# Order of the token-mixing work inside the value projection: PV products one by one, two transposes moved ahead, the short tile fourth of five

## The chip, the core and the metric

The kernel runs on one NeuronCore of one Trainium2 chip. The core has five engines that run side by side and wait for each other by semaphores: TensorE (PE, matrix products, results into PSUM), VectorE (DVE), ScalarE (ACT), GpSimd (POOL) and SyncE (SP, which issues most DMAs). The metric is device time in microseconds (us) of one execution; lower is better.

## The reference

Eight images (b = 0 to 7) of 576 tokens and 512 channels go through three blocks, all in float32:

```python
q_s = exp(q - max(q, -1)); q_s /= sum(q_s, -1) + 1e-9          # per head, over 64 channels
k_s = exp(k - max(k, 2));  k_s /= sum(k_s, 2) + 1e-9           # over the 576 tokens
x   = q_s @ (k_s^T @ v)                                        # (576, 512) per image
h   = gelu_tanh(x @ w_in)                                      # 512 -> 1024
u, v = h[:, :512], h[:, 512:]
v_n = (v - mean) / sqrt(var + 1e-6) * g_ln                     # over the 512 channels
y   = x + (u * (w_sg @ v_n + b_sg)) @ w_out                    # w_sg mixes tokens
t   = y + (y^T @ U @ V)^T                                      # rank 32, over tokens
out = t + relu(t @ w_ch1) @ w_ch2                              # 512 -> 2048 -> 512
```

## The kernel before

Every float32 operand of a product is split into a high part `h` (float32r) and a low rest `l`, and a product is made of three: h·h, h·l, l·h. ACT makes the high part by a copy, DVE or POOL the low part by a subtraction (`low`).

The first three blocks run image by image in one loop over `b`; the last block (`ch1`, `ch2`) runs over 512 columns of all tokens after it. An image's pass has these stages on PE: `emit_xT` (px, four of them: x transposed), `emit_Vh` (pv: the v half of x @ w_in, one tile of 128 tokens each for t = 0 to 3 and a short tile of 64 tokens, t = NT = 4), `emit_Uh` (pu, four: the u half), `emit_S` (pS: token mixing by w_sg), then `emit_kv` and `emit_qT` of the next image and `emit_y` (py). The rank-32 product of an image is not finished in its own pass. Its transposes `emit_yT` (pt, from tile yt) for t = 0 and 1 stand between the px of the next image, and the transposes for t = 2, 3, 4, the product with U (`emit_U`, pp, nine products) and the four products with V (`emit_PV`, pw, two products each) stand inside the pv stage of the next image. So the pv stage of images 1 to 7 holds pieces of the image before.

What follows a pv tile: ACT takes gelu of it (ge), DVE takes mean and variance (`stats`: bn_stats, bn_aggr, add), POOL the power -0.5 (mv), DVE the shift (sh), ACT normalises in place and copies the high part (vh), POOL subtracts the low part (vl). The short tile is computed with high and low rows side by side, so its pv is first copied by ACT, then added by DVE (tile ge, 64 partitions), then put through gelu, and its low part is made by DVE into the other half of vh4. After a pw, DVE adds it to yt, and SP sends yt to DRAM (u2d).

Beside this the key maximum of the next image is found: DVE folds the key tiles (`k_fold`, km, in two halves of two operations), PE transposes km (`k_max`, pm), DVE reduces it (mx, mh, ml), POOL makes two diagonal matrices of it (diag), and PE spreads it over all partitions (`k_spread`, pb, between the second and the third pu); ACT copies that to kmx, DVE subtracts it from the keys, ACT takes exp.

What sets the order: PE's order is the order of the code everywhere. For images 1 to 6 DVE's order is that of the code too; ACT, POOL and SP are ordered ahead of time by a scheduler with a time model of its own. For image 0 DVE, ACT, POOL and SP, and for image 7 ACT, follow the code. On the chip each engine runs its list strictly in that order.

PSUM has eight banks: `ps2` holds three tiles of two banks (tag "big"), handed out in turn to px, pv, pw, pu, pS, py, and to the transposes t = 2 and 3; `ps1` holds two tiles of one bank for the transposes t = 0, 1, 4, for pp, pm, pb and pk. A new tile waits until the one three (or two) places before it in the same pool has been read by its last reader.

Of the kernel before, what the change touches and what calls it, by code (L numbers as in the profile page):

```python
# [22 lines left out]
def fused_kernel(tc, q, k, v, w_in, g_ln, w_sgT, b_sg, w_out, U, V, w_ch1, w_ch2, outT):  # L23
# [4 lines left out]
    NT = S // P  # L28
# [18 lines left out]
    def mm(out, lhsT, rhs, first, last):  # L47
        pe.matmul(out, lhsT, rhs, start=first, stop=last)  # L48
# [456 lines left out]
    vh = {}  # L505
    ln = {}

    def emit_Vh(b, t):
        xh, xl, xr, _ = x_t[b]
        pv = ps2.tile([P, 1024], F32, tag="big", name="pv")[:, 0:F]  # L510
        cols = slice(F, 2 * F)
        for kc in range(NC):
            if t < NT:
                a, l = xh[:, kc, t * P : (t + 1) * P], xl[:, kc, t * P : (t + 1) * P]
                mm(pv, a, wi_h[:, kc, cols], kc == 0, False)
                mm(pv, a, wi_l[:, kc, cols], False, False)
                mm(pv, l, wi_h[:, kc, cols], False, kc == NC - 1)
            else:
                a = xr[:, kc].rearrange("p j r -> p (j r)")
                mm(pv, a, wi_h[:, kc, cols], kc == 0, False)  # L520
                mm(pv, a, wi_l[:, kc, cols], False, kc == NC - 1)
        ge = tmpp.tile([P, F], F32, tag="ge", name="ge", bufs=3)
        ln[b, t] = ge
        if t < NT:
            act.activation(ge, pv, AF.Gelu_apprx_tanh)
        else:
            copy(ge[0:R], pv[64 : 64 + R])
            tt(dve, ge[0:R], pv[0:R], ge[0:R], ALU.add)
            act.activation(ge[0:R], ge[0:R], AF.Gelu_apprx_tanh)
# [11 lines left out]
    def emit_ln(b, t):  # L541
        ge, mv = ln.pop((b, t))
        n = TR[t]
        shift = tmpp.tile([P, 1], F32, tag="sh", name="sh", bufs=4)
        dve.scalar_tensor_tensor(
            out=shift[0:n], in0=mv[0:n, 0:1], scalar=-1.0, in1=mv[0:n, 1:2], op0=ALU.mult, op1=ALU.mult
        )
        act.activation(ge[0:n], ge[0:n], AF.Identity, bias=shift[0:n], scale=mv[0:n, 1:2])
        h = wrk.tile([P, F], F32R, tag=f"vh{t}", name=f"vh{t}")
        if t < NT:  # L550
            l = wrk.tile([P, F], F32R, tag=f"vl{t}", name=f"vl{t}")
            copy(h, ge)
            low(pool, l, ge, h)
            vh[b, t] = (h, l)
        else:
            copy(h[0:R], ge[0:R])
            low(dve, h[64 : 64 + R], ge[0:R], h[0:R])
            vh[b, t] = h
# [58 lines left out]
    def emit_yT(b, t):  # L617
        n = TR[t]
        if t not in (2, 3):
            pt = ps1.tile([P, C], F32, tag="ps1", name="pt1")  # L620
        else:
            pt = ps2.tile([P, 1024], F32, tag="big", name="pt1")[:, 0:C]
        for c in range(NC):
            pe.transpose(pt[0:n, c * P : (c + 1) * P], y_t[b][:, c, t * P : t * P + n], ident)
        h = wrk.tile([P, C], F32R, tag=f"vh{t}", name=f"yh{t}")
        if t < NT:
            l = wrk.tile([P, C], F32R, tag=f"vl{t}", name=f"yl{t}")
            copy(h, pt)
            low(dve, l, pt, h)
            yn[b, t] = (h, l)  # L630
        else:
            copy(h[0:R], pt[0:R])
            low(dve, h[64 : 64 + R], pt[0:R], h[0:R])
            yn[b, t] = (h,)
# [98 lines left out]
    def more(n):  # L733

        for _ in range(n):
            while pieces and len(loaded) < 3:
                loaded.append(pieces.popleft())
                if not loaded[-1].loaded:
                    loaded[-1].load()
            while stores:  # L740
                stores.popleft()()
            if loaded:
                begun.append(loaded.popleft())
                begun[-1].start()
            if len(begun) > 1 or (begun and not loaded and not pieces):
                merged.append(begun.popleft())
                merged[-1].merge()
            if len(merged) > 1 or (merged and not begun):
                merged.popleft().split()
# [13 lines left out]
    spread = [mid] * B  # L763
# [69 lines left out]
    for b in range(B):  # L833
        nxt = b + 1 if b + 1 < B else None
        part = in_order(*order.get(b, (dve,)))
        part.__enter__()

        if not nxt:
            close_att()
            p2a, close_p2a = opened("p2a", side="right")  # L840
            load_u(p2a, 0)
        if nxt:
            load_k(nxt)
            fold = k_fold(nxt)
        for t in range(NT + 1):
            emit_Vh(b, t)
            if nxt:
                with behind(dve):
                    for t2 in ((0, 1), (2, 3), (4,), (), ())[t]:
                        q_max(nxt, t2)  # L850
                    if t in (2, 3):
                        next(fold)
                        next(fold)
            if t < NT:
                stats(b, t)
            more(spread[b][0][t])
            if t > 0:
                emit_ln(b, t - 1)
            if t == NT:
                stats(b, t)  # L860
            if b == 0 and t > 0:
                sum_x(b, t - 1)
            if b > 0:
                for t2 in {0: (2,), 1: (3, 4)}.get(t, ()):
                    emit_yT(b - 1, t2)
            if t == 2 and b > 0:
                for t2 in range(NT + 1):
                    emit_U(b - 1, t2)
            if t in (3, 4) and b > 0:
                for c in range(2 * t - 6, 2 * t - 4):  # L870
                    emit_PV(b - 1, c)

        if nxt:
            k_max(nxt)
        for f in range(NF):
            if nxt and f == 2:
                k_spread(nxt)
            if b == 0:
                more(spread[b][1][f])
            emit_Uh(b, f)  # L880
            if f == 0:
                emit_ln(b, NT)
                if nxt:
                    load_v(nxt)
            if nxt:
                for t in ((0, 1), (2, 3, 4), (), ())[f]:
                    q_sub(nxt, t, pool if b == 0 and t > 1 else dve)
                for t in ((), (), (0, 1), (2, 3, 4))[f]:
                    k_sub(nxt, t)
            if b > 0:  # L890
                more(spread[b][1][f])
            if not nxt and f == 1:
                load_w(p2a, 0)
                split_u(p2a, 0)
        if nxt:
            for t in range(NT + 1):
                q_exp(nxt, t)
            k_exp(nxt)
            for t in range(NT + 1):
                q_sum(nxt, t)  # L900
            q_total(nxt)
            for t in range(NT + 1):
                q_norm(nxt, t, dve if t < 2 else pool)

        for f in range(NF):
            emit_S(b, f)
            if f > 0:
                split_G(b, f - 1)
            if f == NF - 1:
                split_G(b, f)  # L910
            if not nxt and f == NF - 1:
                close_wi()
                p2b, close_p2b = opened("p2b", 3, side="right")
                for fc in (1, 2):
                    load_w(p2b, fc)

                def early(fc):
                    ch1(0, fc, ps2.tile([P, 1024], F32, tag="big", name="ph")[:, 0:BLK], p2b)

                early(0)  # L920
            more(spread[b][2][f])
        if nxt:
            emit_kv(nxt)
            emit_qT(nxt, 0)
            emit_qT(nxt, 1)
            norm_kv(nxt)
        for c in range(NC):
            more(spread[b][3][c])
            emit_y(b, c)
            if nxt and 0 < c < 3:  # L930
                emit_qT(nxt, 1 + c)
                if c == 2 and b + 2 < B:
                    load_q(b + 2)
        if nxt:
            emit_xT(nxt, 0)
            emit_xT(nxt, 1)
            emit_yT(b, 0)
            emit_xT(nxt, 2)
            emit_yT(b, 1)
            emit_xT(nxt, 3)  # L940
        else:
            early(1)
            more(99)
            for t in range(NT + 1):
                emit_yT(b, t)
            for t in range(NT + 1):
                emit_U(b, t)
            early(2)
            for c in range(NC):
                emit_PV(b, c)  # L950
        if b < B - 1:
            part.__exit__(None, None, None)
# [75 lines left out]
```

## Time and profile before

| | |
|---|---|
| median of 3 runs | 1430.74 us (1428.48 to 1434.74) |
| the profiled execution | 1432.9 us |
| its span, first to last instruction | 1431.1 us |
| PE busy | 1370.5 us, 96% of the span |
| DVE, ACT, POOL busy | 631.9, 485.2, 348.9 us |
| mean granted TensorE clock | 0.981 of full speed |

The profiled execution is 1.8 us longer than its span and 2.2 us above the median. Images 0 to 7 take the first 645 us or so of the span, the last block the rest. A busy PE counts overlapping products, so PE's losses are read from the starts of its instructions: back to back, products of 512 columns start 0.23 us apart.

### The profile page before, as it was taken

To read this page: it belongs to the slowest core of one execution; us is meant where nothing else is said; L and a number is where in the kernel's file an instruction comes from. 1 tells how busy PE (TensorE), PEld (TensorE's weight loads), DVE (VectorE), ACT (ScalarE), POOL (GpSimd) and SP (SyncE) were. 2 spreads that over 40 slices of the span, in tenths; PEclk is the share of its full clock that TensorE was granted. 3 is DMA by queue.
4 is the path that set the end of the run, shared out by engine and by line. 5 is a ranking of instruction groups with operands and counts; after the bars stand their busy time and mean duration, and the time that the engine had idled before them with its cause. 6 is when DMAs were issued, how large, how long until landed. Compare 5 with 4: busy or idle time off the path is not lost.

```text
span 1431.1 us, 19023 instructions
## 1 busy us (share of the span) xinstructions
PE 1370.5 (96%) x7672; PEld 1180.5 (82%) x7672; DVE 631.9 (44%) x1140; ACT 485.2 (34%) x838; POOL 348.9 (24%) x384
## 2 busy tenths in 40 slices
PE   3688999999999999998999999999999999999998
PEld 2488898989898988897888888888888888888887
DVE  6787868686868687654521111112111111111111
ACT  3455757575757565522411111111111111111110
POOL 5864343434343334423400001010010100101000
PEclk8789999999999999999999999999999999999999
DMA  7324333323232422448210010101001010010000
GB/s 244 104 83 125 92 118 90 125 82 124 84 125 83 125 82 90 143 148 297 75 59 0 0 60 0 59 1 40 20 0 59 0 60 0 1 59 1 30 0 30
DMA packets 72056, 104.42 MB, mean 73 GB/s; under 512 B 5920, under 2 KB 34592, under 8 KB 71968
## 3 DMA queue, kind: packets, MB, share of 16 engines
q1 hardware_dynamic: 69088, 92.72, 20.4%
q0 software_dynamic: 2880, 10.49, 2.2%
q8 instruction: 60, 0.98, 0.3%
q14 instruction: 28, 0.23, 0.0%
HBM read 73.83 MB, written 29.36 MB: 72 GB/s over the span
## 4 chain that ended last, share of the span: by engine, by line
PE 82%; DVE 6%; ACT 4%; DMA 3%; POOL 2%; issue 2%; SPq 0%; ACTq 0%; DVEq 0%; POOLq 0%
PE acc L48 27%; PE ph L48 27%; PE pS L48 7%; PE py L48 7%; PE pv L48 5%; PE pu L48 5%; DMA stg<-in_w_ch_dram 1%; PE pt L453 1%; PE pk L48 1%; PE pp L48 1%; ACT xh L57 1%; ACT x L57 1%; DMA u2d<-yt 1%; DVE stg L173 1%; POOL qt L51 1%
## 5 line engine op out<-in xcount | busy, mean ns | idle before, releaser
L48 PE MATMUL acc<-hh,w 128*128 128x512 f32 x1152 | 379.3, 390 | 0.0
L48 PE MATMUL ph<-uh,w 128*128 128x512 f32 x1152 | 378.1, 389 | 0.0
L706 DVE SCALAR_TENSOR_TENSOR hl<-ph,hh 128x512 fp32r<-128x512 f32 x144 | 99.4, 691 | 569.5 <-ACT hh L705 569.5
L705 ACT ACTIVATE hh<-ph 128x512 fp32r<-128x512 f32 x144 | 86.0, 597 | 639.7 <-PE ph L48 639.7
L48 PEld LDWEIGHTS acc<-hh,w 128*128 128x128 f32 x1152 | 217.1, 188 | 45.2
L48 PEld LDWEIGHTS ph<-uh,w 128*128 128x128 f32 x1152 | 216.5, 188 | 45.0
L48 PE MATMUL acc<-hl,w 128*128 128x512 f32 x576 | 225.2, 391 | 4.0 <-DVE hl L706 4.0
L48 PE MATMUL ph<-ul,w 128*128 128x512 f32 x576 | 224.1, 389 | 0.0
L51 POOL TENSOR_TENSOR ul<-u,uh 128x512 fp32r<-128x512 f32 x32 | 40.6, 1300 | 566.4 <-ACT uh L57 566.4
L48 PEld LDWEIGHTS acc<-hl,w 128*128 128x128 f32 x576 | 108.7, 189 | 26.9 <-DVE hl L706 4.4
L48 PEld LDWEIGHTS ph<-ul,w 128*128 128x128 f32 x576 | 108.0, 188 | 22.4
L174 ACT ACTIVATE f<-stg 128x256 f32<-128x256 f32 (+2 forms) x91 | 39.2, 434 | 68.9 <-DVE stg L173 30.7
L48 PE MATMUL py<-gh,wo_h 128*128 128x288 f32 x256 | 57.9, 308 | 2.9 <-DVE gt L590 2.9
L48 PE MATMUL pu<-xh,wi_h 128*128 128x288 f32 x256 | 57.5, 307 | 2.1 <-DVE yt L51 2.1
L48 PE MATMUL pv<-wi_h,xh 128*128 128x512 f32 x128 | 53.0, 414 | 3.6 <-ACT xh L57 3.6
L48 PE MATMUL pu<-xh,wi_l 128*128 128x288 f32 x256 | 55.9, 300 | 0.6 <-POOL wi_l L51 0.6
L48 PE MATMUL pv<-wi_h,xl 128*128 128x512 f32 x128 | 52.6, 411 | 3.7 <-DVE xl L51 3.7
L48 PE MATMUL pu<-xl,wi_h 128*128 128x288 f32 x256 | 55.9, 300 | 0.0
L48 PE MATMUL py<-gh,wo_l 128*128 128x288 f32 x256 | 55.8, 300 | 0.0
L48 PE MATMUL py<-gl,wo_h 128*128 128x288 f32 x256 | 55.7, 300 | 0.0
L48 PE MATMUL pS<-sg_h,vh 128*128 128x288 f32 x256 | 54.8, 296 | 0.3 <-ACT ut L570 0.3
L48 PE MATMUL pS<-sg_h,vl 128*128 128x288 f32 x256 | 54.7, 295 | 0.0
(148 smaller groups left out, 2206.9 us busy)
## 6 DMA issues: line engine op xcount, KB each, us to landing
stg<-in_w_ch_dram SPq DMA_DIRECT2D x64, 256.0 KB, 2.6
wd<-chw SPq DMA_DIRECT2D x40, 256.0 KB, 2.9
w<-wd POOLq DMA_DIRECT2D x20, 512.0 KB, 7.2
u2d<-yt SPq DMA_DIRECT2D x32, 288.0 KB, 2.1
u<-u2d SPq DMA_DIRECT2D x9, 1024.0 KB, 5.3
out_dram<-res SPq DMA_DIRECT2D x36, 256.0 KB, 2.1
vt<-in_v_dram SPq DMA_DIRECT2D x32, 256.0 KB, 6.7
qt<-in_q_dram SPq DMA_DIRECT2D x7, 1024.0 KB, 6.2
```

Of the source, the lines that this page charges most:

```text
L48: pe.matmul(out, lhsT, rhs, start=first, stop=last)
L51: return eng.tensor_tensor(out=out, in0=a, in1=b, op=op)
L57: act.activation(out, src, AF.Copy)
L173: eng.tensor_scalar(out=hi, in0=hi, scalar1=F64_MOST, scalar2=-F64_MOST, op0=ALU.min, op1=ALU.max)
L174: act.activation(t, hi, AF.Prelu, scale=F64_SCALE, alpha=F64_SIGN)
L453: pe.transpose(pt[:, t * P : t * P + n], qt[0:n, t, c * P : (c + 1) * P], ident[0:n, 0:n])
L705: act.activation(a, ph, AF.Relu)
L706: dve.scalar_tensor_tensor(out=l, in0=ph, scalar=0.0, in1=as_f32(a), op0=ALU.max, op1=ALU.subtract)
```

## The change

In the pv stage of images 1 to 7 (image 0 keeps its order): the transposes t = 2 and t = 4 come before the first pv instead of after it; t = 3 comes after the first pv, and the U product after the second. The pv tiles are taken in the order 0, 1, 2, short, 3. The four pw were two pairs, one before and one after the short tile; now pw0 stands before the short tile, pw1 after it, and pw2 and pw3 stand inside the last pv, between its channel blocks. The normalisation (`emit_ln`) of the short tile, which was inside the first pu, comes before `k_max`, and that of tile 3 takes its place.

```diff
-    def emit_Vh(b, t):
+    def emit_Vh(b, t, between=None):
...
         for kc in range(NC):
+            if between and kc > 1:
+                between(kc)
...
-        for t in range(NT + 1):
-            emit_Vh(b, t)
-            if nxt:
+        if b > 0:
+            for t in (2, NT):
+                emit_yT(b - 1, t)
+        for i, t in enumerate(range(NT + 1) if b == 0 else (0, 1, 2, NT, 3)):
...
+            emit_Vh(b, t, (lambda kc: emit_PV(b - 1, kc)) if b > 0 and i == NT else None)
+            if nxt and i != 3:
+                ahead_of()
+            if b > 0 and i in (2, 3):
+                emit_PV(b - 1, i - 2)
             if t < NT:
                 stats(b, t)
-            more(spread[b][0][t])
-            if t > 0:
-                emit_ln(b, t - 1)
+            more(spread[b][0][i])
+            if i > 0:
+                emit_ln(b, (0, 1, 2, NT, 3)[i - 1] if b else t - 1)
...
-            if b > 0:
-                for t2 in {0: (2,), 1: (3, 4)}.get(t, ()):
-                    emit_yT(b - 1, t2)
-            if t == 2 and b > 0:
+            if b > 0 and i == 0:
+                emit_yT(b - 1, 3)
+            if b > 0 and i == 1:
                 for t2 in range(NT + 1):
                     emit_U(b - 1, t2)
-            if t in (3, 4) and b > 0:
-                for c in range(2 * t - 6, 2 * t - 4):
-                    emit_PV(b - 1, c)
...
-                emit_ln(b, NT)
+                emit_ln(b, 3 if b else NT)
```

How this stands on the engines, at three places of image 1 (the other images up to 6 are alike). PE, at the change from px to pv; pt1 is a transpose of yt, before:

```order
L48 MATMUL px_1336<-qh_1104,kh_1128 128x288 x2
L48 MATMUL px_1336<-ql_1105,kh_1128 128x288 x2
L48 MATMUL px_1336<-qh_1104,kl_1129 128x288 x2
L48 MATMUL pv_1354<-wi_h_109,xh_1284 128x512
L48 MATMUL pv_1354<-wi_l_110,xh_1284 128x512
L48 MATMUL pv_1354<-wi_h_109,xl_1285 128x512
```

The same place of PE now:

```order
L48 MATMUL px_1336<-ql_1105,kh_1128 128x288 x2
L48 MATMUL px_1336<-qh_1104,kl_1129 128x288 x2
L626 MATMUL pt1_1354<-ident_95,yt_1143 128x128 x4
L626 MATMUL pt1_1363<-ident_95,yt_1143 64x128 x4
L48 MATMUL pv_1371<-wi_h_109,xh_1284 128x512
L48 MATMUL pv_1371<-wi_l_110,xh_1284 128x512
```

The first of the two transposes is a "big" tile, so it takes the PSUM place that the first pv had (px_1298's), and the first pv takes the next one, that of px_1317.

DVE, from the low part of the rank-32 sum (pst) to the sum of the short tile (ge with 64 partitions) or the first PV addition (yt<-pw), before:

```order
L51 TENSOR_TENSOR pst_1476<-pp_1466,pst_1476 32x512
L51 TENSOR_TENSOR km_1450<-km_1450,kt_1351 128x512
L51 TENSOR_TENSOR km_1450<-km_1450,kt_1351 64x512
L535 BN_STATS bst_1496<-ge_1492 128x6
L536 BN_AGGR mv_1497<-bst_1496 128x2
L537 TENSOR_SCALAR mv_1497<-mv_1497 128x1
L545 SCALAR_TENSOR_TENSOR sh_1502<-mv_1454 128x1
L51 TENSOR_TENSOR yt_1143<-pw_1509,yt_1143 128x576
L51 TENSOR_TENSOR yt_1143<-pw_1514,yt_1143 128x576
L51 TENSOR_TENSOR ge_1528<-pv_1519,ge_1528 64x512
```

The same stretch of DVE now:

```order
L51 TENSOR_TENSOR pst_1444<-pp_1434,pst_1444 32x512
L375 TENSOR_REDUCE qm_1386<-qt_106 64x8
L51 TENSOR_TENSOR km_1463<-kt_1351 128x512
L51 TENSOR_TENSOR km_1463<-km_1463,kt_1351 128x512
L51 TENSOR_TENSOR yt_1143<-pw_1466,yt_1143 128x576
L537 BN_STATS bst_1471<-ge_1460 128x6
L538 BN_AGGR mv_1472<-bst_1471 128x2
L539 TENSOR_SCALAR mv_1472<-mv_1472 128x1
L547 SCALAR_TENSOR_TENSOR sh_1477<-mv_1422 128x1
L51 TENSOR_TENSOR km_1463<-km_1463,kt_1351 128x512
L51 TENSOR_TENSOR km_1463<-km_1463,kt_1351 64x512
L51 TENSOR_TENSOR ge_1495<-pv_1486,ge_1495 64x512
```

The last query maximum (qm) and the first half of the key fold (km) were ahead of pst; they now stand behind it, and both halves stand ahead of the short tile's sum.

DVE, up to the reduction of the transposed key maximum (mx), before:

```order
L545 SCALAR_TENSOR_TENSOR sh_1542<-mv_1497 128x1
L535 BN_STATS bst_1549<-ge_1528 64x6
L536 BN_AGGR mv_1550<-bst_1549 64x2
L537 TENSOR_SCALAR mv_1550<-mv_1550 64x1
L51 TENSOR_TENSOR yt_1143<-pw_1555,yt_1143 128x576
L51 TENSOR_TENSOR yt_1143<-pw_1560,yt_1143 128x576
L335 TENSOR_REDUCE mx_1570<-pm_1565 128x4
```

The same stretch of DVE now:

```order
L537 BN_STATS bst_1542<-ge_1540 128x6
L538 BN_AGGR mv_1543<-bst_1542 128x2
L539 TENSOR_SCALAR mv_1543<-mv_1543 128x1
L173 TENSOR_SCALAR stg_1170<-stg_1170 128x256
L180 TENSOR_SCALAR f32_1215<-f32_1215 128x256
L181 SCALAR_TENSOR_TENSOR f32_1215<-stg_1132,f32_1215 128x256
L547 SCALAR_TENSOR_TENSOR sh_1558<-mv_1512 64x1
L51 TENSOR_TENSOR vh4_1561<-ge_1495,vh4_1561 64x512
L335 TENSOR_REDUCE mx_1569<-pm_1564 128x4
```

The short tile's shift (sh, 64 partitions) and its low part (vh4) came after mx; they now come before it, with the statistics of tile 3 and a weight conversion (stg, f32). ACT makes the high part that this low part waits for, and there the order is the same before and now: shift and scale of the short tile, gelu of the first pu (ut), copy to vh4, gelu of the second pu.

## Rows read from the trace of the kernel before

**Rows 1.** The page's first part: busy time of each engine.
```profile
PE 1370.5 (96%) x7672; PEld 1180.5 (82%) x7672; DVE 631.9 (44%) x1140; ACT 485.2 (34%) x838; POOL 348.9 (24%) x384
```
**Rows 2.** The page's second part: granted TensorE clock in 40 slices.
```profile
PEclk8789999999999999999999999999999999999999
```
**Rows 3.** Waits of PE over the whole span: total us, times, longest.
```profile
PE pu L48 <- DVE yt L51: 2.1, 7, 0.6
PE pv L48 <- ACT ge L525: 1.5, 7, 0.2
```
**Rows 4.** Timeline of PE, image 1: start us, us, engine, line, operation, count, wait.
```profile
138.72 0.40 PE L48 MATMUL pv<-wi_h,xh 128*128 128x512 f32 x1
...
140.83 0.39 PE L48 MATMUL pv<-wi_h,xh 128*128 128x512 f32 x1
141.06 0.40 PE L48 MATMUL pv<-wi_l,xh 128*128 128x512 f32 x1
141.93 0.50 PE L48 MATMUL pv<-wi_h,xl 128*128 128x512 f32 x1 [0.48 <-DVE xl L51]
142.27 0.60 PE L624 MATMUL pt<-ident,yt 128*128 128x128 f32 x4
142.62 0.48 PE L48 MATMUL pv<-wi_h,xh 128*128 128x512 f32 x1
...
156.73 1.20 PE L48 MATMUL pw<-v_w,pst 128*128 128x288 f32 x4
157.76 0.60 PE L333 MATMUL pm<-ident,km 128*128 128x128 f32 x4
158.31 0.54 PE L48 MATMUL pu<-xh,wi_h 128*128 128x288 f32 x2
...
165.31 0.79 PE L48 MATMUL pb<-diag,ones 128*128 128x512 f32 x2
165.94 0.43 PE L48 MATMUL pu<-xh,wi_h 128*128 128x288 f32 x2
```
**Rows 5.** Timeline of DVE, image 1.
```profile
139.55 0.76 DVE L51 TENSOR_TENSOR xl<-px,xh 128x576 fp32r<-128x576 f32 x1 [0.40 <-ACT x L57]
...
150.72 0.69 DVE L535 BATCH_NORM_STATS2 bst<-ge 128x6 f32<-128x512 f32 x1
...
152.00 0.70 DVE L51 TENSOR_TENSOR pst<-pp,pst 32x512 fp32r<-32x512 f32 x1
152.73 1.41 DVE L51 TENSOR_TENSOR km<-km,kt 128x512 f32<-128x512 f32 x2
...
157.57 0.68 DVE L51 TENSOR_TENSOR ge<-pv,ge 64x512 f32<-64x512 f32 x1 [0.23 <-ACT ge L57]
...
162.55 0.67 DVE L335 TENSOR_REDUCE mx<-pm 128x4 f32<-128x512 f32 x1
...
166.63 0.69 DVE L51 TENSOR_TENSOR vh<-ge,vh 64x512 fp32r<-64x512 f32 x1 [2.08 <-ACT vh L57]
```
**Rows 6.** Timeline of ACT, image 1.
```profile
151.31 0.60 ACT L57 ACTIVATE pst<-pp 128x512 fp32r<-128x512 f32 x1 [0.84 <-PE pp L48]
...
165.43 0.65 ACT L570 ACTIVATE ut<-pu 128x576 f32<-128x576 f32 x1
165.98 0.62 ACT L57 ACTIVATE vh<-ge 64x512 fp32r<-64x512 f32 x1
```
**Rows 7.** Timeline of DVE, image 0: its key fold.
```profile
62.13 1.02 DVE L51 TENSOR_TENSOR km<-kt 128x512 f32<-128x512 f32 x1
63.18 1.78 DVE L51 TENSOR_TENSOR km<-km,kt 128x512 f32<-128x512 f32 x1
```
**Rows 8.** Timeline of POOL, the same stretch of image 0.
```profile
62.56 3.66 POOL L51 TENSOR_TENSOR sg_l<-sgs,sg_h 128x576 fp32r<-128x576 f32 x2
```
**Rows 9.** Timeline of PE, image 0, where its py products begin.
```profile
117.51 0.82 PE L48 MATMUL py<-gh,wo_h 128*128 128x288 f32 x2 [2.90 <-DVE gt L590]
```
**Rows 10.** Busy us by stretch: PE, PEld, DVE, ACT, POOL, then granted clock.
```profile
117.50:123.40 5.90, 5.89 (x24) 5.90 (x25) 5.66 (x13) 2.51 (x6) 0.79 (x1) 0.50 0.28 90
```

More of the change, by code (lines that the diff above doesn't have):

```diff
@@ L844, in fused_kernel, with ahead_of @@
             fold = k_fold(nxt)
-        for t in range(NT + 1):
-            emit_Vh(b, t)
-            if nxt:
+        if b > 0:
+            for t in (2, NT):
+                emit_yT(b - 1, t)
+        for i, t in enumerate(range(NT + 1) if b == 0 else (0, 1, 2, NT, 3)):
+            def ahead_of(i=i):
                 with behind(dve):
-                    for t2 in ((0, 1), (2, 3), (4,), (), ())[t]:
+                    for t2 in ((0, 1), (2, 3), (4,), (), ())[i]:
                         q_max(nxt, t2)
-                    if t in (2, 3):
+                    if i in (2, 3):
                         next(fold)
                         next(fold)
+            if nxt and i == 3:
+                ahead_of()
+            emit_Vh(b, t, (lambda kc: emit_PV(b - 1, kc)) if b > 0 and i == NT else None)
+            if nxt and i != 3:
+                ahead_of()
+            if b > 0 and i in (2, 3):
+                emit_PV(b - 1, i - 2)
             if t < NT:
                 stats(b, t)
-            more(spread[b][0][t])
-            if t > 0:
-                emit_ln(b, t - 1)
+            more(spread[b][0][i])
+            if i > 0:
+                emit_ln(b, (0, 1, 2, NT, 3)[i - 1] if b else t - 1)
             if t == NT:
```

## The prediction

> **What bounds the kernel now.** I read the busy shares first: PE is busy for 96% of the span [rows 1], so only what moves PE's instructions counts, and any wait of PE in the change's stage is lost whole unless a later wait takes it up. Next the list of PE's waits: in each of images 1 to 7 there is one wait for a gelu in front of the short tile and one for a PV addition inside the pu [rows 3]. Then the timeline of one image, which the other five with a next image repeat [rows 4]. The reader should see how a wait is priced there. Products of 512 columns start 0.23 us apart (140.83, 141.06). The one that waits for xl starts 0.87 behind its forerunner though only 0.48 is shown as idle, and what follows it starts 0.34 later. So a wait costs its shown idle, plus 0.16 for the pipeline to run out, plus 0.11 to refill: idle + 0.27. Last the timelines of DVE and ACT beside it [rows 5, 6], since they release PE. The clock stays at full speed from the fifth slice to the seventeenth, where images 1 to 7 lie [rows 2].
>
> **What the change takes away**, per image of 1 to 6.
> - The xl wait: 0.48 + 0.27 = 0.75.
> - The gelu wait in front of the short tile: 1.5 / 7 = 0.21 [rows 3], + 0.27 = 0.48.
> - The second group of four pw takes 1.03 (156.73 to 157.76) [rows 4]. Two pu take 7.00 (158.31 to 165.31) less the wait inside them, 2.1 / 7 + 0.27 = 0.57 [rows 3]: 6.43 for 48 products of 288 columns, 0.134 each. Four need 0.53; lost 0.50.
> - That wait in the pu itself: 0.57.
> - pb takes 0.63 to the next pu where two products need 0.45 to 0.46: 0.18.
>
> Together 2.48 us, in six images 14.9.
>
> **What it puts in their place**, per image, each with its bounds.
>
> (a) *The first pv.* After the last px (PE is free at 138.72) come two sets of transposes, 0.35 each (142.27 to 142.62) and 0.09 of switching: PE reaches the first pv at 139.5. But the first pv now needs the PSUM place of the third px, and DVE reads that until xl ends at 139.55 + 0.76 = 140.31 [rows 5]. So the moved transposes cover the last xl wait and open another one ahead: 140.36 - 139.5 = 0.86, + 0.11 = 0.97. Bounds 0 (place free earlier) and 0.97.
>
> (b) *pw2, inside the last pv.* It needs the PSUM place of the short tile, free when DVE has added that tile's two halves. Counted from the end of the U product on PE, the ACT copy of pst ends at 0.80 (0.20 + 0.60) [rows 6]; then DVE does, in its order, pst 0.73, the query maximum 0.6, two km 1.35, a PV addition 0.67 (as xl), statistics and shift 1.28 (150.72 to 152.00), two km 1.35 and the addition 0.68 [rows 5]: 7.5. PE needs 12 pv, pw0, 8 short pv, pw1 and 6 pv: 26 x 0.23 + 4 x 0.134 = 6.5. It waits 1.0, + 0.11 = 1.1.
>
> On top of this, POOL's first vl becomes ready within 0.1 of the first km, since both follow pst by a short chain: ACT normalises and copies in about the time that DVE takes for pst and one maximum. In image 0 the trace shows what such a meeting does. The second km of a pair, 0.69 when alone (1.41 for two), took 1.78 while POOL subtracted sg_l [rows 7, 8]: 1.1 more on DVE. In the pv stage of before, POOL's vl came only when no km was left behind it. I count the meeting: (b) is 2.2. Bounds 0 (addition ready at once) and 2.3.
>
> The Trainium skill bears on this place: SBUF — State Buffer, section "Who interferes with whom", says that a DVE instruction with two SBUF inputs and a GpSimd instruction that reads SBUF exclude each other, and that the one that comes second is blocked for the other's whole length. The km row agrees with it: 1.78, against 0.69 alone. By that rule the sum below holds its 1.1 per image; without it, it does not.
>
> (c) *The first pu* now needs the place of the last pv, which stands directly ahead of pm. Its gelu is out 0.16 + 0.05 + 0.60 + 0.05 = 0.86 after the last product was issued, pm covers 0.55 (157.76 to 158.31): 0.31 + 0.11 = 0.42. Bounds 0 and 0.9.
>
> (d) *pb.* This is the largest term. pb needs POOL's diagonals, these need mx on DVE, and mx now stands behind the short tile's vh4 on DVE. That low part needs the ACT copy to vh4, and that copy stands behind the gelu of the first pu, which cannot start before the first pu is done, 3.21 + 0.21 = 3.42 after its start. From the start of that gelu the rows give the chain: copy 0.55 later (165.43 to 165.98), low part 0.65 later (166.63), mx 0.72 after that, and from mx to the third pu, through both diagonals and pb, 3.39 (162.55 to 165.94). That is 5.31, so the third pu starts no earlier than 3.42 + 5.31 = 8.73 after the first one; without a wait it would be 6.43 + 0.45 = 6.88. Lost 1.85. Before, mx waited for nothing of the first pu, and PE reached pb last. Bounds: 1.85 below, if the order holds; 3.0 above, if the shift of the short tile comes 0.7 late behind the tile 3 statistics and the weight conversion, and POOL's second diagonal meets a subtraction on DVE for 0.5. I take 1.85.
>
> What hides the rest: the later normalisation of tile 3 and its vl on POOL are needed by the fourth group of the first pS, behind two more pu (6.4); the key exponentials come about 2 us later and are needed after four pS, some 14 us on; the gelu of the third pu may be late by about 3 us before its place is missed. The four u2d transfers now stand together in SP's queue ahead of one weight load, which is used a stage later. These I count at nothing; with their cover gone they would cost what they are late.
>
> **Sum.** (a) to (d) are 0.97 + 2.2 + 0.42 + 1.85 = 5.44 per image, against 2.48: +2.96, in six images +17.8. Image 7 has no km, pm or pb. It loses the waits for xl (0.75), gelu (0.48) and the longest pu wait (0.6 + 0.27 [rows 3]), 2.1, and pays (a) and (c), the latter without pm's cover, 1.9: counted as 0, bounds -2 and +2. Image 0 is untouched. The profiled execution would go from 1432.9 to 1450.7; it lies 2.2 above the median of the runs, so in those terms 1430.7 + 17.8 = 1448.5.
>
> **The clock.** A wait of 2.90 in image 0 was followed by a half-speed stretch [rows 9, 10]: 24 products took 5.9 where 24 x 0.134 = 3.2 would do, 2.7 lost. The waits of up to 0.48 in images 1 to 6 were not [rows 2, 4]. The new ones, (b) near 2.1 and (d) near 1.9 with a product in between, lie between, nearer to 2.90, but below it. I take two falls in the six images, 5.4; bounds none and one in each, 16.2. That makes 1448.5 + 5.4 = 1454; I put 1453.
>
> **The rivals.**
> - *No meeting of km and vl, no fall.* ACT could be some 0.7 us later than I think, so that vl comes after the km pair. Then (b) is 1.1, the sum +1.86 x 6 = 11.2: 1442. Against it: both chains start at the same pst.
> - *A fall in every image.* 1448.5 + 16.2 = 1464.7. For it: each image has two waits of about 2 us within some 12 us. Against it: no wait as short as these is seen to bring a fall. The Trainium skill's page TensorE: Matmul & The Clock Gate, section "HAM oscillation — how this bites in real kernels", describes a loop that pays for the slow clock in every pass because each pass waits; rows 9 and 10 show one such fall, and none of before's images 1 to 6 shows a repetition.
> - *The pb chain is early* (not slower). If DVE's low part of the short tile did not wait for the gelu of the first pu, mx would come as before and (d) be near 0; with (b) at 1.1 the sum is 0.97 + 1.1 + 0.42 - 2.48 = 0.0: 1431. Its place is pb, its price 1.85 x 6 = 11, and it decides if the chain is 1.85 shorter than read. Against it: it stands so on both engines' lists.
> - *All waits vanish* (faster). The removed 14.9 + 2.1 = 17.0 stay gone and the PSUM places are free in time: 1430.7 - 17.0 = 1414. For it: DVE has four of ten parts idle here. Against it: (a) alone is read from one row. In part this is the rival that the change doesn't do what it says: transposes in front cover the last xl only if the first pv can start behind them.
>
> **How the numbers follow.** Forecast (meeting, none to four falls, 1446 to 1459): 0.42. No meeting, no fall (1437 to 1446): 0.22. A fall in every image: 0.16. pb early: 0.10. All waits gone: 0.10. A measurement tells this kernel from itself to about 0.5%, 7 us, so slower means above 1438: 0.42 + 0.16 + nearly all of 0.22 = 0.79; same 0.11; faster 0.10. The range reaches from 1436, below the second case, to 1467, above the third, and leaves out the two last cases, 2 in 10.
>
> **What would show it.** In the new trace: PE waits at pb for POOL's diag in each of images 1 to 6, and the third pu starts 8.7 or more after the first; (a) a wait of the first pv for DVE's xl; (b) a wait at the second or third pw for the DVE sum ge, and a km of about 1.7 beside a vl; (c) a wait of the first pu for the gelu. The xl wait at the last product of a tile and the wait inside the first two pu are gone. Falls show as half-speed slices. I am wrong if pb starts right behind the second pu, if PE's waits of images 1 to 6 sum to less than before, or if the time moves although these waits do not: then something outside the stage did it.

## The result, and the profile after

The changed kernel takes 1448.3 us (median of 4 runs, 1447.06 to 1449.24) against 1430.72 before. The recorded ratio of the runs is 1.0117, 95% interval 1.0104 to 1.0130; the two medians by themselves give 1.0123. The forecast was 1453 (1436 to 1467), slower. The profiled run took 1449.24, 16.3 more than that of before, in a span of 1447.5. In the page, PE has 2.7 us more busy time in a span 16.4 longer, so most of the loss is waiting [rows 1]; no slice shows a low clock after the third, as before [rows 2].

The page after, busy time and granted clock:

```profile
PE 1373.2 (95%) x7672; PEld 1184.3 (82%) x7672; DVE 638.6 (44%) x1140; ACT 468.5 (32%) x826; POOL 359.4 (25%) x384
PEclk9889999999999999999999999999999999999999
```

PE's waits after (total us, times, longest):

```profile
PE pb L48 <- POOL diag L51: 14.5, 14, 3.1
PE pw L48 <- DVE ge L51: 8.0, 6, 1.3
PE pv L48 <- DVE xl L51: 3.7, 7, 0.5
...
PE acc L48 <- DVE hl L708: 2.5, 3, 1.6
```

The two waits of [rows 3] are gone from this list. Two waits take their place, about five times as long in total: pb for a diagonal (twice in each image; 3.4 of the 14.5 us stood there before too) and pw for the short tile's addition. PE's timeline of image 1, to be laid beside [rows 4]:

```profile
139.31 1.10 PE L626 MATMUL pt<-ident,yt 128*128 128x128 f32 x8
140.94 0.50 PE L48 MATMUL pv<-wi_h,xh 128*128 128x512 f32 x1 [0.53 <-DVE xl L51]
...
155.70 0.40 PE L48 MATMUL pv<-wi_h,xl 128*128 128x512 f32 x1
157.43 0.53 PE L48 MATMUL pw<-v_w,pst 128*128 128x288 f32 x2 [1.33 <-DVE ge L51]
...
159.44 0.60 PE L333 MATMUL pm<-ident,km 128*128 128x128 f32 x4
160.06 0.53 PE L48 MATMUL pu<-xh,wi_h 128*128 128x288 f32 x2
...
167.53 0.50 PE L48 MATMUL pb<-diag,ones 128*128 128x512 f32 x1 [0.82 <-POOL diag L51]
169.04 0.50 PE L48 MATMUL pb<-diag,ones 128*128 128x512 f32 x1 [1.02 <-POOL diag L51]
169.38 0.42 PE L48 MATMUL pu<-xh,wi_h 128*128 128x288 f32 x2
```

The first pu starts at 160.06, the third at 169.38: 9.32 us, where before they were 7.63 apart (158.31 and 165.94). DVE, ACT and POOL beside it, to be laid beside [rows 5, 6]. First DVE:

```profile
151.93 1.67 DVE L51 TENSOR_TENSOR km<-km,kt 128x512 f32<-128x512 f32 x1
...
155.37 1.40 DVE L51 TENSOR_TENSOR km<-km,kt 128x512 f32<-128x512 f32 x2
156.71 0.67 DVE L51 TENSOR_TENSOR ge<-pv,ge 64x512 f32<-64x512 f32 x1
...
159.26 1.40 DVE L51 TENSOR_TENSOR yt<-pw,yt 128x576 f32<-128x576 f32 x2
...
164.74 0.69 DVE L51 TENSOR_TENSOR vh<-ge,vh 64x512 fp32r<-64x512 f32 x1 [2.15 <-ACT vh L57]
165.46 0.69 DVE L335 TENSOR_REDUCE mx<-pm 128x4 f32<-128x512 f32 x1
...
166.47 1.02 DVE L547 SCALAR_TENSOR_TENSOR sh<-mv 128x1 f32<-128x1 f32 x1
167.41 4.47 DVE L51 TENSOR_TENSOR qt<-qt,qm 128x512 f32<-128x512 f32 x5
```

ACT, the gelu of the last pv, then the first gelu of a pu and the copy behind it:

```profile
159.88 0.60 ACT L527 ACTIVATE ge<-pv 128x512 f32<-128x512 f32 x1
...
163.55 0.65 ACT L572 ACTIVATE ut<-pu 128x576 f32<-128x576 f32 x1
164.09 0.62 ACT L57 ACTIVATE vh<-ge 64x512 fp32r<-64x512 f32 x1
```

POOL:

```profile
151.30 1.75 POOL L51 TENSOR_TENSOR vl<-ge,vh 128x512 fp32r<-128x512 f32 x1 [1.72 <-ACT vh L57]
...
166.44 1.04 POOL L51 TENSOR_TENSOR diag<-ident,mh 128x512 fp32r<-128x512 f32 x1 [3.96 <-DVE mh L338]
167.44 1.56 POOL L51 TENSOR_TENSOR diag<-ident,ml 128x512 fp32r<-128x512 f32 x1
```

The chain reads from one list to the next: ut, vh on ACT, the second half of vh and mx on DVE (which stands idle 2.15 us in front of it), the two diagonals on POOL, pb, third pu.

A slice is 36 us long and hides short changes of the clock. The stretch behind pb in images 1 and 2, taken by itself (columns as in [rows 10]):

```profile
166.50:170.00 3.50, 1.66 (x9) 1.10 (x8) 3.50 (x5) 3.23 (x5) 3.50 (x3) 1.00 0.00 0
243.47:246.88 3.41, 3.41 (x14) 3.31 (x15) 2.88 (x5) 3.40 (x7) 2.08 (x2) 0.50 0.22 77
```

In images 2, 4 and 6 a half-speed stretch (1.2 GHz) begins at the second pb, in 1, 3 and 5 there is none. Below such a stretch is called a fall of the clock. In image 2 it makes the third and fourth pu take 7.73 us instead of 6.39, 1.34 more; over the whole stage images 2, 4 and 6 are 1.42 longer than 3 and 5.

Where the 16.3 us went, by the start times in PE's timeline. From the first px to the first pS an image takes 37.72 on the mean of images 1 to 6 before and 41.32 after: 21.6 us in all, of which three falls of the clock are 4.3 and the new waits less the old ones 17.3. Image 7 takes 35.05 instead of 38.27 (-3.2), and the last block is 2.0 shorter: before, a half-speed stretch from 669.5 to 676.4 followed a wait of 4.0 us for hl; after, that wait is 1.6 and the clock stays up. As far as the traces show, that is chance and not the change: over all traces of this document the last block takes 812.1 to 816.2 us, and no edit reaches it. The rest cancels: image 0 is 0.6 longer, and from the first pS to the next px images 1 to 6 are 0.5 shorter in all.

### The profile page after: what moved, and what is told of

Same layout as the page of the kernel before. It is cut to its first block, busy times and chain, and to the rows that moved or that the text cites. A ratio compares the mean times of both kernels' runs of the same rounds, so it can differ in the third digit from the quotient of the medians.

```text
span 1447.5 us, 18989 instructions
## 1 busy us (share of the span) xinstructions
PE 1373.2 (95%) x7672; PEld 1184.3 (82%) x7672; DVE 638.6 (44%) x1140; ACT 468.5 (32%) x826; POOL 359.4 (25%) x384
## 4 chain that ended last, share of the span: by engine, by line
PE 79%; DVE 8%; issue 3%; DMA 3%; ACT 3%; POOL 3%; SPq 0%; POOLq 0%; ACTq 0%; DVEq 0%
PE ph L48 25%; PE acc L48 25%; PE pS L48 8%; PE py L48 8%; PE pu L48 4%; PE pv L48 3%; DMA stg<-in_w_ch_dram 2%; DVE km L51 2%; PE pt L453 1%; PE pk L48 1%; PE pp L48 1%; DVE yt L51 1%; ACT xh L57 1%; DVE bst L537 1%; ACT x L57 1%
## 5 line engine op out<-in xcount | busy, mean ns | idle before, releaser
L48 PE MATMUL pS<-sg_l,vh 128*128 128x288 f32 x256 | 54.7, 295 | 0.0
```

## The experiments

The theory: PE loses at two places, at pb, because mx stands behind vh4 in DVE's queue, and at the third pw, because the short tile's addition stands behind the key fold in the same queue. The main rival: the time goes with PE's new order itself, or with POOL's queue, and DVE's order has no part in it. All ratios are against the kernel before, on the same chip. The table holds times read from PE's timeline, means of images 1 to 6 in us.

| kernel | ratio (95%) | px to first pS | first to third pu | pS to next px | image 7, px to pS |
|---|---|---|---|---|---|
| before | 1 | 37.72 | 7.62 | 33.80 | 38.27 |
| after | 1.0117 (1.0104 to 1.0130) | 41.32 | 9.45 | 33.71 | 35.05 |
| ln back | 1.0014 (1.0002 to 1.0026) | 38.19 | 6.95 | 34.11 | 35.08 |
| diagonal on DVE | 1.0070 (1.0056 to 1.0083) | 39.52 | 8.37 | 34.21 | 35.04 |
| fold early | 1.0102 (1.0076 to 1.0128) | 41.26 | 9.33 | 33.77 | 35.04 |
| both (ln back, fold early) | 0.9982 (0.9971 to 0.9992) | 37.36 | 6.95 | 34.08 | 35.00 |
| two in front | 1.0001 (0.9992 to 1.0011) | 37.99 | 7.62 | 33.90 | 38.11 |
| one in front | 1.0033 (1.0020 to 1.0046) | 38.27 | 6.95 | 34.16 | 34.75 |
| max first | 1.0000 (0.9989 to 1.0012) | 37.43 | 6.96 | 34.28 | 34.75 |
| image 7 only | 0.9984 (0.9973 to 0.9995) | 37.75 | 7.62 | 33.77 | 35.93 |
| PV apart | 0.9973 (0.9960 to 0.9987) | 37.23 | 7.35 | 33.51 | 36.83 |
| apart and image 7 | 0.9953 (0.9937 to 0.9970) | 37.23 | 7.35 | 33.52 | 35.05 |
| addition first | 0.9970 (0.9959 to 0.9981) | 37.51 | 8.25 | 33.51 | 35.02 |

**The layer norm tail back.**

```diff
-            if i > 0:
+            if i > 0 and not (b and i == NT):
                 emit_ln(b, (0, 1, 2, NT, 3)[i - 1] if b else t - 1)
...
-                emit_ln(b, 3 if b else NT)
+                emit_ln(b, NT)
+                if b:
+                    emit_ln(b, 3)
```

> The changed kernel, with one part undone: from image 1 on, the layer norm tail of the short token tile (DVE's sh and the second half of vh4, ACT's ln and copy) is issued behind k_max again and not in front of it. Theory: the wait of pb for the diagonals comes from DVE's mx standing behind vh4's low part, which stands behind ACT's copy behind the first ut. With it gone, first pu to third pu goes from 9.3-9.6 us back to about 7.0 in images 1 to 6 (-2.4 x 6 = -14.5), the second diagonal takes 1.0 instead of 1.56, and the half-speed stretch behind pb in images 2, 4, 6 goes too (-1.34 x 3 = -4.0): 1448.3 - 18.5 = 1430 us (1427 to 1436). Rival: pb waits because of POOL's own queue or because the order on PE (two early transposes, U earlier) leaves less time between pm and pb; then DVE's order does nothing and the time stays at 1446 to 1450.

Measured: 1434.2 us, ratio 1.0014. First to third pu 6.95, no half-speed stretch in images 1 to 6, px to pS 18.7 us shorter in six images where 18.5 were expected. (The median fell by 14.1 only; the traced execution, 1431.56, is the shortest of ten.) PE's timeline of image 1, and POOL's and DVE's:

```profile
164.83 0.62 PE L48 MATMUL pb<-diag,ones 128*128 128x512 f32 x2
```

```profile
162.71 1.04 POOL L51 TENSOR_TENSOR diag<-ident,ml 128x512 fp32r<-128x512 f32 x1
```

```profile
165.10 3.08 DVE L51 TENSOR_TENSOR qt<-qt,qm 128x512 f32<-128x512 f32 x5
```

pb waits no more; the second diagonal takes 1.04 instead of 1.56, and the five qt subtractions that it met take 3.08 instead of 4.47. The rival falls: PE's and POOL's order are as in the changed kernel. The 2.4 us by which pS to px grew (0.40 an image) stand in front of the third pS. This trace names no releaser for it, but it starts 0.06 behind the end of ACT's gelu ut (178.72 + 0.65 to 179.43); in the next run ut is named. The scheduler changed ACT's order in both.

**The second diagonal on DVE.**

```diff
-        for eng, w in ((pool if b else dve, mh), (pool if b else dve, ml)):
+        for eng, w in ((pool if b else dve, mh), (dve, ml)):
```

> The changed kernel, with the second of the two diagonals of k_max (the one of the low part) built on DVE in place of POOL, in images 1 to 7; all orders stay. Theory: the second diagonal is late because it queues behind the first on POOL and then meets DVE's qt subtraction (1.56 us beside 1.04). On DVE it stands right behind ml and both are done about 1.0 to 1.5 us earlier: -6 to -9 in six images, and part of the half-speed stretches goes (0 to -4): 1435 to 1442 us, first pu to third pu 8.0 to 8.5. Rival: the two diagonals meet each other on the shared SBUF port, DVE's or POOL's then takes 1.6 to 2 us, and nothing is won: 1446 to 1450.

Measured: 1443.36, first to third pu 8.37. The wait of 1.02 is gone, that of 0.82 stays, and no fall of the clock follows it. The two diagonals do meet (1.44 on DVE beside POOL's 1.04), but the later end is still earlier:

```profile
166.94 1.04 PE L48 MATMUL pb<-diag,ones 128*128 128x512 f32 x2 [0.82 <-POOL diag L51]
```

```profile
166.00 1.44 DVE L51 TENSOR_TENSOR diag<-ident,ml 128x512 fp32r<-128x512 f32 x1
```

px to pS fell by 10.8 in six images, as much as the theory's two parts together, but 3.0 came back behind the first pS, most of it where the third pS waits for ut, and the last block was 3.0 longer. So the mechanism was as expected, and the time misses its bound by 1.4.

**The key fold early.**

```diff
-                    if i in (2, 3):
+                    if i in ((1, 3) if b else (2, 3)):
                         next(fold)
                         next(fold)
```

> The changed kernel, with the first pair of the key fold's four DVE instructions one token tile earlier (behind the second PV-side tile, ahead of its statistics, where DVE stands idle 0.87 us in front of pst). Theory: PE's 1.33 us in front of the third pw are DVE's queue in front of the short tile's ge addition (km 0.67 + 1.67 beside POOL's vl, yt, statistics, km 1.40); with a pair out of it the addition comes 0.7 to 1.2 us earlier: -4 to -7 in six images, 1441 to 1444 us, and the km of the pair takes 0.7 instead of 1.67. Rival: the addition waits for ACT's copy of the upper half (ends 154.74) or for the PSUM place, and the pair's place means nothing: 1447 to 1450. A loss is possible too, if pst moves later by more than 0.9 us and the first pw waits: 1450 to 1454.

Measured: 1447.85, no gain, and yet the theory's wait did go:

```profile
158.03 0.53 PE L48 MATMUL pw<-v_w,pst 128*128 128x288 f32 x2 [0.34 <-DVE ge L51]
```

```profile
150.47 0.69 DVE L51 TENSOR_TENSOR km<-km,kt 128x512 f32<-128x512 f32 x1
```

The pw wait is 0.34 instead of 1.33 and the km 0.69 instead of 1.67. First pv to first pu is 18.28 instead of 19.12: 5.0 in six images. What ate it is the clock. With the same two waits at pb, 0.82 and 1.01 to 1.02, the half-speed stretch now stands behind pb in all six images of the traced execution, the first of them here:

```profile
170.46:173.87 3.41, 3.41 (x15) 3.34 (x14) 2.87 (x5) 3.40 (x7) 2.08 (x2) 0.50 0.22 77
```

The third and fourth pu take 7.9 in each image, 1.53 more: 9.2 where the changed kernel loses 4.3. This was in neither theory, so the next run tries the early pair without the wait at pb. The trace is one execution: the four spread from 1442.42 us at a mean granted clock of 0.982 to 1452.62 at 0.976, and the traced one is the last. So the number of falls probably differs between executions of this kernel too; only one was traced.

**Both edits.** The diffs of the layer norm tail back and of the key fold early together.

> The changed kernel with two edits: the short tile's layer norm tail back behind k_max and the first pair of the key fold one tile earlier. Theory: the earlier pair takes 1.0 us off the wait for the short tile's ge addition and gives 0.2 back at the first pu (pv to first pu 19.12 -> 18.28 us); alone that was hidden, since in that run a half-speed stretch of 1.5 us stood behind pb in all six images. Without a wait at pb no such stretch comes, and px to pS is 38.2 - 0.85 = 37.4: -5.1 in six images against the kernel with the first edit alone (ratio 1.0014): ratio 0.998 (0.996 to 1.000). Rival: the earlier pair is worth nothing by itself (the time moves to the next wait, pb or the second pS): ratio 1.001 to 1.003.

Measured: 1428.34, ratio 0.9982. px to pS is 37.36, 0.83 below the kernel with the tail back, and no half-speed stretch stands in images 1 to 6. The early pair is worth 5 us where the clock does not take them. The changed kernel with two details of its order mended is thus a little faster than the one before.

**Two transposes in front, alone** (on the kernel before).

```diff
+        if b > 0:
+            for t in (2, NT):
+                emit_yT(b - 1, t)
         for t in range(NT + 1):
...
-                for t2 in {0: (2,), 1: (3, 4)}.get(t, ()):
+                for t2 in {1: (3,)}.get(t, ()):
```

> The kernel before, with one part of the change alone: the transposes of tiles 2 and 4 (the short one) of the last image's y in front of the first pv; tile 3 stays behind the second. Theory (term a): the first pv's 0.75 us wait for xl goes, but it now waits about 0.97 for the PSUM place that xl frees, so +0.2 an image: 1430.7 + 1.3 = 1432 us (1430 to 1434). Rival: the two transposes lie in the wait for xl and nothing takes its place: -0.75 x 6 = 1426 us.

Measured: 1432.69 against 1432.98, ratio 1.0001. px to pS is 0.27 longer an image, where 0.22 was expected. One wait takes the other's place.

**One transpose in front** (on the kernel with both edits).

```diff
-            for t in (2, NT):
-                emit_yT(b - 1, t)
+            emit_yT(b - 1, NT)
...
             emit_Vh(b, t, ...)
+            if b > 0 and i == 0:
+                for t2 in (2, 3):
+                    emit_yT(b - 1, t2)
             if nxt and i != 3:
                 ahead_of()
...
-            if b > 0 and i == 0:
-                emit_yT(b - 1, 3)
```

> The kernel with both edits, and of the transposes only the short tile's in front of the first pv; those of tiles 2 and 3 stand behind it. Theory (term a): the first pv then takes the PSUM place of an earlier px and does not wait 0.53 + 0.45 for the one that the third xl frees; it waits for the last xl instead, 0.75 less the 0.33 that one transpose fills: -0.5 us in seven images, ratio 0.9955 (0.993 to 0.998). Rival: the two transposes behind the first pv make the second pv wait for the first one's gelu, or U for yl, by as much as is won: ratio as with both edits, 0.997 to 0.999.

Measured: 1436.24, a miss: px to pS is 0.90 longer than with both edits. The first pv came earlier as expected (4.98 behind px, 5.75 with two). But the two yl now stand ahead of the query maxima on DVE, which waits for ACT's copies:

```profile
146.35 1.29 DVE L51 TENSOR_TENSOR yl<-pt,yh 128x512 fp32r<-128x512 f32 x2 [1.34 <-ACT yh L57]
```

```profile
154.19 0.53 PE L48 MATMUL pw<-v_w,pst 128*128 128x288 f32 x2 [0.54 <-DVE pst L51]
...
159.01 0.53 PE L48 MATMUL pw<-v_w,pst 128*128 128x288 f32 x2 [0.80 <-DVE ge L51]
```

**The maxima first again.** The added block of the last diff stands behind `ahead_of()`.

> The kernel with one transpose in front, with one edit: the first two maxima of q (DVE's qm) stand ahead of the two yl in DVE's queue again. Theory: that kernel was slow since DVE stood idle 1.34 us at the first yl, with qm behind it, so that pst came 1.2 us late and the first pw waited 0.54 and the third 0.80. With qm in that gap both waits go: px to pS 38.25 -> 36.9 us, 0.45 less than with two transposes in front, ratio 0.996 (0.995 to 0.9975). Rival: pst is late because tiles 2 and 3 reach U's chain later through ACT's copies, whatever DVE's order: px to pS stays above 37.8, ratio 1.000 to 1.003.

Measured: ratio 1.0000, px to pS 37.43. The first pw waits no more, so DVE's order was the cause of that. The third still waits, 1.01 where with both edits it waits 0.35. The rows of ACT and DVE account for most of the 0.66:

```profile
156.05 0.81 ACT L550 ACTIVATE ge<-ge,sh,mv 128x512 f32<-128x512 f32 x1 [1.42 <-DVE sh L547]
156.89 0.59 ACT L57 ACTIVATE ge<-pv 64x512 f32<-64x512 f32 x1
```

```profile
155.46 0.56 DVE L547 SCALAR_TENSOR_TENSOR sh<-mv 128x1 f32<-128x1 f32 x1
155.94 1.40 DVE L51 TENSOR_TENSOR km<-km,kt 128x512 f32<-128x512 f32 x2
157.51 0.68 DVE L51 TENSOR_TENSOR ge<-pv,ge 64x512 f32<-64x512 f32 x1 [0.18 <-ACT ge L57]
```

ACT's scheduled list puts a normalisation in front of the short tile's copy, so the addition waits 0.18 for it. The shift sh takes 0.56 beside a vl of POOL (154.71 to 156.00), where it took 0.15 with both edits, and pushes the key fold and the addition behind it back by 0.41.

Neither expectation holds whole. In the stage it equals the kernel with both edits; its profile is longer in image 0 and in the last block, which the edit does not reach.

**The new order in image 7 alone.** The old loop for images 1 to 6, the changed one for the last.

```diff
+        new = b == B - 1
...
-        for i, t in enumerate(range(NT + 1) if b == 0 else (0, 1, 2, NT, 3)):
+        for i, t in enumerate((0, 1, 2, NT, 3) if new else range(NT + 1)):
...
```

> The changed kernel's order in the last image (image 7) alone; images 1 to 6 keep the order of before. Theory: in image 7 no next key is folded and no pb is waited for, so the removed waits count there with nothing in their place: first px to first pS 38.27 -> 35.05 us, and the time is that of the kernel before less 3.2: ratio 0.9978 (0.996 to 0.999), some 1429 to 1430 us on this chip where before is 1433. The last block's time moves by where a half-speed stretch falls in it (0 to -1.8) and not by the change. Rival: the gain in image 7 is eaten in the last block, since its first weights and words come at their own time: ratio 0.9995 to 1.0005.

Measured: 1428.92 against 1431.2, ratio 0.9984, within what the theory gave. px to pS is 35.93; the 0.9 more than after is a first pv that comes 6.63 behind px, not 5.75.

**The PV products apart, alone** (on the kernel before).

```diff
-            emit_Vh(b, t)
+            emit_Vh(b, t, (lambda kc: emit_PV(b - 1, kc - 1)) if b > 0 and t == NT else None)
...
-                for c in range(2 * t - 6, 2 * t - 4):
-                    emit_PV(b - 1, c)
+                emit_PV(b - 1, 3 * t - 9)
```

> The kernel before with one part of the change alone: the four PV products (pw) apart, the first behind the fourth token tile, the second and third within the short tile's products, the fourth behind them; token tiles, transposes and U stay. Theory: the 0.5 us that the second four matmuls waited and most of the first pu's 0.57 go, as the sum of the prediction has it (0.50 + 0.57 an image): -0.9 x 7 = -6, ratio 0.996 (0.994 to 0.998). Rival: DVE's y additions then stand ahead of the short tile's ge addition, and PE or the pm-to-pb chain waits for that instead: ratio 0.999 to 1.003.

Measured: 1427.35, ratio 0.9973. In the stage -0.49 an image where -0.9 was expected, and -0.28 more behind the first pS; image 7 is 1.44 shorter. This part alone is a gain; the rest of what was expected is kept back by a new wait at the third pw:

```profile
156.16 0.53 PE L48 MATMUL pw<-v_w,pst 128*128 128x288 f32 x2 [0.82 <-DVE yt L51]
```

**Both parts that gain.** The last two edits together.

> The kernel before with the PV products apart in images 1 to 6 and the changed kernel's order in image 7 alone. The two gains lie in different images, so they add: 0.9973 with the products apart (image 7 at 36.83 us there), less 36.83 - 35.9 to 35.05 = 0.9 to 1.8 us: ratio 0.996 to 0.997. Rival: the changed order in image 7 needs the changed order in image 6's last pass (the two transposes come from there) and gives nothing more: ratio 0.9973 to 0.998.

Measured: 1424.43 us against 1432.06, ratio 0.9953 (0.9937 to 0.9970), the lowest of all, though its interval meets those of the products apart and of the next run. The gains add, by the stage times: 37.23 in images 1 to 6 as with the products apart, 35.05 in image 7 as in the changed kernel.

**The addition first** (on that kernel).

```diff
+            if t == 3 and b > 0 and not new:
+                emit_PV(b - 1, 0)
             if t < NT:
                 stats(b, t)
...
-            if t in (3, 4) and b > 0 and not new:
-                emit_PV(b - 1, 3 * t - 9)
+            if t == NT and b > 0 and not new:
+                emit_PV(b - 1, 3)
```

> The kernel with the PV products apart and image 7 in the new order, with one edit: DVE's addition for the first pw stands ahead of the fourth token tile's statistics, not behind them. Theory: the third pw's 0.82 us is DVE's queue (it waits for ACT's gelu 0.59 us, then runs the statistics, then the addition that frees the third pw's PSUM place); the addition comes 1.6 us earlier and the wait goes: px to pS 37.2 -> 36.4, ratio lower by 0.82 x 6 / 1431 = 0.0034 than without the edit: 0.993 (0.992 to 0.995). Rival: the fourth tile's statistics come 0.7 us later and something behind them (the short tile's addition, pm to pb) takes it back: no difference from the kernel without the edit, 0.996 to 0.997.

Measured: ratio 0.9970, no gain: in the stage 0.28 an image longer, in the ratio worse by less than the intervals tell apart. The wait at the third pw is gone, first pv to first pu fell from 19.53 to 18.91, and first to third pu rose from 7.35 to 8.25, at pb again:

```profile
168.50 0.50 PE L48 MATMUL pb<-diag,ones 128*128 128x512 f32 x1 [0.30 <-POOL diag L51]
169.49 0.50 PE L48 MATMUL pb<-diag,ones 128*128 128x512 f32 x1 [0.50 <-POOL diag L51]
```

The rival's mechanism holds: what DVE does earlier for one wait, it does later for the other.

## Why the prediction was right

| step | predicted, us an image | measured | shown by |
|---|---|---|---|
| (a) first pv waits for xl's place | 0.97 | 0.95 | image 1 after; two in front alone |
| (b) third pw waits for the addition | 2.2 | 2.0 | image 1 after; fold early, both edits |
| (c) first pu waits for the gelu | 0.42 | 0.07, not for the gelu | image 1 after, both edits |
| (d) pb behind vh4 and mx | 1.85 | 2.44 | image 1 after; tail back |
| less the waits removed | 2.48 | 2.48 assumed | not measured one by one |
| sum of six images | 17.8 | 17.3 | 21.6 less the falls |
| falls of the clock | 2 of 2.7 | 3 of about 1.4 | windows behind pb, stage times |
| image 7 | 0 | -3.2 | image 7 alone |

- *(a)* was sized from one row of DVE and holds. PE has the transposes out by 139.31 + 0.79 = 140.10 and starts the first pv at 140.94, + 0.11 to refill.
- *(b)* holds with the meeting. The km took 1.67 while POOL's vl ran from 151.30 to 153.05, as the step took over from image 0 [rows 7, 8]. By the rule of the Trainium skill that the step named (SBUF — State Buffer, "Who interferes with whom"), the one that comes second waits out the other, and the km ends 0.55 after vl. Its pair alone takes 1.40. Not all of the 2.0 is at the third pw: 1.6 is there (1.33 + 0.27), and 0.4 is a wait of the pv behind the second pw, which starts at 154.44, 0.55 behind that pw, where 0.26 is usual.
- *(c)* was wrong in its mechanism: the first pu does not need the place of the last pv. In image 1 it starts at 160.06, while ACT reads that pv from 159.88 to 160.48. It starts behind the first of DVE's two additions from 159.26 on, that of the third pw, and where the third pw comes earlier, it waits for this addition by name. With both edits:

```profile
157.89 0.53 PE L48 MATMUL pu<-xh,wi_h 128*128 128x288 f32 x2 [0.54 <-DVE yt L51]
```

  The section on the kernel says that places are handed out in turn; this pu got the place of the third pw instead. Why the pool gave it that one, no run shows. The loss is 0.07: from pm to the first pu are 0.62 us after and 0.55 before.
- *(d)* has its mechanism right and came out midway between its bounds. One of the upper bound's two reasons is what happened: the second diagonal met a subtraction on DVE and took 1.56 instead of 1.04. With the tail back the whole of it is gone.
- *The sum* is right to 0.5 (17.3 by the stage times; the four measured steps less 2.48 give 17.9), in part by luck: (c) was too high by 0.35 and (d) too low by 0.59.
- *The clock*: the number of falls and their price were both off, in opposite directions, 5.4 against 4.3. The half-speed stretch behind the wait of 2.90 in image 0 is longer than those behind pb [rows 9, 10]. The rival of a fall in every image did not come here, but it came in the traced execution of the fold early. What decides it is not the wait alone: the changed kernel has both kinds of images, with waits that agree to 0.1.
- *Image 7* failed too: -3.2, outside its bounds (-2 to +2). I charged it (a) and (c) and counted three waits as removed. (c) does not occur: its first pu starts before the gelu of the last pv does. And I left out that before, in this image alone, the U product waits for the last transposes, which now come earlier.

```profile
607.65 0.42 PE L48 MATMUL pu<-xh,wi_h 128*128 128x288 f32 x2
608.58 0.60 ACT L527 ACTIVATE ge<-pv 128x512 f32<-128x512 f32 x1
```

  That is after. U's waits before:

```profile
580.48 0.50 PE L48 MATMUL pp<-yh,u_w 128*128 128x512 f32 x1
581.21 0.49 PE L48 MATMUL pp<-yl,u_w 128*128 128x512 f32 x1 [0.22 <-DVE yl L51]
581.92 0.50 PE L48 MATMUL pp<-yh,u_w 128*128 128x512 f32 x1 [0.22 <-DVE yh L51]
```

  They start 0.52, 0.73 and 0.71 behind their forerunners instead of 0.23: with the refill 1.4 in all, gone after. They stand unchanged in the run with the products apart alone, which takes 1.44 off image 7; so the products apart are less than half of the 3.2.
- *The total.* Image 7 (-3.2), the last block (-2.0, by chance) and the clock (-1.1) are why 1448.3 lies under 1453; that the sum came so near rests on (b) and (d), read right, and on errors that partly cancel.
- The rival that the pb chain is early is refuted by [rows 5] and the new trace: DVE stood idle 2.15 in front of vh. So is the one that all waits vanish. *No meeting* is refuted by the km of 1.67, against 0.69 in the run with the fold early.

Open is why the same waits bring a fall in every second image of one traced execution and in every image of another; no run separates it, and of each kernel one execution was traced. That the meeting is about 1.0 of (b) (1.67 less 0.69) is read from the rows and not tried apart: the early fold takes the meeting and a part of the queue away together.

## What to carry to other kernels

Where an engine with a strict list has little slack, moving one piece of work forward moves a wait, here between the third pw and pb: follow each released tile to the next thing that stands behind it in that list before counting a gain. A change of several parts is worth taking apart: two parts of this one gain 0.5% together, and one detail, a short tile's tail placed in front of a maximum, cost 1%. Which PSUM place a tile gets is worth reading from who releases it, not from a count of turns. A wait that a trace shows as gone may still bring nothing, if the clock falls oftener; compare stage times, not waits.

## What the runs showed of the hardware

- A DVE instruction that POOL blocks waited to the end of POOL's, small as it was. The shift sh has one element in each partition and takes 0.15 alone; beside POOL's first diagonal it took 1.02 and ended at 167.49, with the diagonal (167.48).
- The blocking goes both ways and costs both: five qt subtractions took 4.47 and the diagonal 1.56 where they met, 3.08 and 1.04 where they did not.
- A wait of 0.82 at pb alone was followed by no half-speed stretch in six images (the second diagonal on DVE); 0.82 and 1.02 with a product in between were followed by one in three images of six, and in six of six in the traced execution of another kernel. The wait of 1.33 at the third pw was followed by none.
